# Attention and GEGLU on one core: 88 warm-up products of 32 columns, a block-diagonal v for batch 0, and clears moved between weight loads

## The chip, the core and the metric

The kernel runs on one core of a Trainium2 chip. A core has TensorE (PE, matrix products; its weight loads are listed as PEld), VectorE (DVE), ScalarE (ACT), GpSimd (POOL) and SyncE (SP), and 16 DMA engines that serve the queues of SP, ACT and POOL. The metric is the device time of one execution in microseconds (us), lower is better; the median over several executions is compared.

## What is computed

Dilated or plain sliding-window attention over 8 batches, 8 heads, 576 positions and head size 64, and then a feed-forward block with GELU gating. The second part takes the attention's output as 4608 tokens of 512.

```python
scores = scale * np.matmul(q, k.transpose(0, 1, 3, 2))
mask_plain = (rel >= 0) & (rel < 32)
mask_dil = (rel >= 0) & (rel < 32 * 4) & (rel % 4 == 0)
masks = np.stack([mask_plain if h < H // 2 else mask_dil for h in range(H)], axis=0)
attn = softmax(np.where(masks, scores, -1e9))
x = np.matmul(attn, v)            # as (4608, 512)
g = x @ w_gate                    # 512 -> 1536
val = x @ w_val
out = gelu(g) * val @ w_out       # 1536 -> 512
```

The first four heads have the plain window, the last four the dilated one. Inputs and output are float32; the kernel computes in float16 with float32 sums.

## The kernel before

**Pairs.** Two heads share the 128 partitions: 64 rows of keys of one head above 64 of the other. A batch has four pairs; pairs n = 0 and 1 of batch 0 are plain, 2 and 3 dilated. For each pair a fixed list of steps exists, named by one letter in the program strings: `S` scores on PE, `P` exp on ACT (line 466), `M` mask on DVE (471, not for batch 0, which has biases instead), `D` denominators on PE with a block-diagonal matrix of ones, `N` numerators on PE with v, `T` and `B` (reciprocal of the denominators by DVE transposes, 550 to 567) or `A` (the same on ACT as log and exp, 559 and 561), and `X`, the product of numerator and reciprocal on DVE (580), which writes the transposed tokens xT. `S1@6` is pair 1's scores in PSUM bank 6; the second number of `D` and `N` chooses one of two windows in PSUM.

**Block-diagonal or half.** For batches 1 to 7, k and v are spread into tiles whose 128x128 blocks are diagonal in the two heads, so that one full product serves both heads. Such a tile's other halves are cleared once (`zero`, line 194, two halves, each one memset of 64x576 float32) and stay clear; the casts (`cast_v`, line 249) write only the diagonal halves. There are three v tiles, `vraw[0..2]`, used by batch modulo 3, and two q/k tiles, by batch modulo 2. Batch 0 is short of time, so its pairs use plain, dense k and v, and each block takes two half products on 64 rows and 64 columns (L434 for S, L528 for N).

**The head.** Before the feed-forward's stream can begin, batch 0's attention runs alone. q and k of the plain heads are loaded (L654), cast (`c0` to `c3`, L351), turned on PE (`t0` to `t7`, L366 and L369) and copied back by DVE or ACT. Ahead of that PE runs `warm` (L637): 60 products of 64 columns on a tile of ones, and then six bias products (`bias_first`, L413) into banks 4 and 6. `b2` and `b3` are the bias products of pairs 2 and 3. `W` stands for filler products of 512 columns on ones (L643). The order of the steps on every engine is written by hand in `gates[0]`: each engine takes its share of it in that order. `G` loads ACT's GELU table; a number pops so many products of the feed-forward's list.

**The feed-forward.** 4608 tokens go in nine chunks of 512. Per chunk PE makes 12 blocks of gate and value (L589, 4 products each), ACT does the GELU (`g`, L743), DVE the product (`u`, L748), and then PE makes four output blocks (L596), stored by L607 or L609. Attention of later batches is woven into the output half of the chunks. Batch 1 is turned on PE (`t8` to `t15`) during chunk 0.

**POOL's queue.** POOL issues the loads of batch 0's dilated heads (L175) and v (`v_first`, L314 and L319), which come as float16 straight from a casting DMA; plain v of batch 0 comes as float32 through SP into `stage` (L237) and is cast by `cast_v_first`, one 128x576 copy for each of two groups g. Then POOL issues the weights: `load_w` (L152, two loads a part, six parts) and `load_wo` (L155). In `second()` (line 678) it goes on with part 4, batch 1's plain q and k (L682, "six"), part 5, its dilated q and k (L175, "eights"), the three output weights, then builds masks (L329 to L336, L132) and clears tiles of batch 1. Its further work for batch 1 (L266, spread of k) is queued behind that. `second_v()` clears the tiles of later batches.

Of the kernel before, what the change touches and what calls it, by code (L numbers as in the profile page):

```python
# [21 lines left out]
def kernel(  # L22
# [10 lines left out]
    nc = tc.nc  # L33
    B, H, S, D = q.shape
# [3 lines left out]
    NHP = H // 2  # L38
# [43 lines left out]
    vraw = [const.tile([P, 4 * NB2 * P], F16, tag=f"v{i}", name=f"v{i}") for i in range(3)]  # L82
# [64 lines left out]
    def load_w(*parts):  # L147

        for i in parts:
            for t, w in ((wg_t, moe_w_gate), (wv_t, moe_w_val)):  # L150
                src = w[:, WC[i][0] : WC[i][1]].rearrange("(kc p) n -> p kc n", p=P)
                nc.gpsimd.dma_start(out=t[i], in_=src)  # L152
# [24 lines left out]
    def blocks(t, plain):  # L177

        return t[:, (1 - plain) * 2 * NB2 * P : (2 - plain) * 2 * NB2 * P].rearrange("p (e c) -> p e c", c=P)

    def views(b):

        raw = qraw[b % 2]
        kt = raw[:, 1280 + 8 * NCL :]
        return (
            raw[:, 0:1280].rearrange("p (g c) -> p g c", g=2),
            raw[:, 1280 : 1280 + 8 * NCL].rearrange("p (g r i) -> p g r i", g=2, r=4),
            blocks(kt, 1),
            blocks(kt, 0),
            blocks(vraw[b % 3], 1),  # L190
            blocks(vraw[b % 3], 0),
        )

    def zero(t, eng=nc.gpsimd, half=(0, 1)):

        for x in half:
            part = t[64 * x : 64 * x + 64].bitcast(F32)
            eng.memset(part[:, :, 32 - 32 * x : 64 - 32 * x], 0.0)

    def st_of(i):  # L200
        return stage[:, 1280 * i : 1280 * i + 1280]
# [44 lines left out]
                in_=rows_[:, S - 64 : S].rearrange("g p d -> p g d"),  # L246
            )

    def cast_v(dst, i):
        st = st_of(i)[:, 0:1152].rearrange("p (e d) -> p e d", d=D)  # L250
        for g in range(2):
            at = slice(NB2 * g, NB2 * g + NB2)
            for x in range(2):
                half = slice(64 * x, 64 * x + 64)
                nc.gpsimd.tensor_copy(dst[half, at, half], st[half, at])  # L255
# [52 lines left out]

    def v_first(g):

        dst = vraw[0][:, 1152:2304].rearrange("p (e d) -> p e d", d=D)
        for x in range(2):
            half = slice(64 * x, 64 * x + 64)
            nc.gpsimd.dma_start(  # L314
                out=dst[half, 8 * g : 8 * g + 8].rearrange("p (i r) d -> p i (r d)", r=4),
                in_=v[0, HK + 2 * g + x, 0 : 4 * P].rearrange("(i p r) d -> p i (r d)", i=2, r=4),
            )
            if g == 0:
                nc.gpsimd.dma_start(out=dst[half, 16:18], in_=v[0, HK + x : H : 2, S - 64 : S].rearrange("g p d -> p g d"))  # L319

    def cast_v_first(eng, g):
        at = slice(576 * g, 576 * g + 576)
        copy(eng, vraw[0][:, at], st_of(0)[:, at])

    def two_masks():
        for x in range(2):
# [15 lines left out]
    def is_plain(n):  # L342
        return pair(n) < NHP // 2

    def copy(eng, dst, src):
        if eng == "act":
            nc.scalar.copy(dst, src)
        elif eng == "pool":
            nc.gpsimd.tensor_copy(dst, src)
        else:  # L350
            nc.vector.tensor_copy(dst, src)  # L351
# [130 lines left out]
    def two_mms(n, w0, lhs_of):  # L482

        mms = []
        pt = tiles["P", n]
        if lhs_of is None:
            groups = []
            for par in range(2):
                bl = two_blocks(n)
                bl = bl[par::2] if is_plain(n) else bl[4 * par : 4 * par + 4]  # L490
                for _, c0, t0, w in bl:
                    for o, l in cuts(w0 + t0, w):
                        p0, q0 = c0 + o, w0 + t0 + o
                        g = groups[-1] if groups else None
                        if g and g[2] == l and g[1] // 512 == q0 // 512 and g[4] == par:
                            last = g[3][-1]
                            if len(g[3]) == 1 or (
                                p0 - last[0] == last[0] - g[3][-2][0] and q0 - last[1] == last[1] - g[3][-2][1]
                            ):
                                g[3].append((p0, q0))  # L500
                                continue
                        groups.append((p0, q0, l, [(p0, q0)], par))
            for p0, q0, l, at, _ in groups:
                k = len(at)
                dp, dq = (at[1][0] - p0, at[1][1] - q0) if k > 1 else (l, l)
                mms.append((q0, at2(psf, q0, [[dq, k], [1, l]]), two_ones, at2(pt, p0, [[dp, k], [1, l]])))
        else:
            for e, c0, t0, w in two_blocks(n):
                for o, l in cuts(w0 + t0, w):
                    q0 = w0 + t0 + o  # L510
                    mms.append((q0, psf[:, q0 : q0 + l], lhs_of(e), pt[:, c0 + o : c0 + o + l]))
        if not is_plain(n):
            r = 0
            while r < 4:
                q0 = w0 + NCL * r + P
                k = sum((w0 + NCL * s + P) // 512 == q0 // 512 for s in range(r, 4))
                rest = two_ones if lhs_of is None else lhs_of(None)
                rhs = pt[:, LD - BK + 16 * r : LD - BK + 16 * (r + k)].rearrange("p (r i) -> p r i", i=16)
                mms.append((q0, at2(psf, q0, [[NCL, k], [1, 16]]), rest, rhs))
                r += k  # L520
        seen = set()
        for q0, o, lhs, rhs in mms:
            st = q0 // 512 not in seen
            seen.add(q0 // 512)
            if n < NHP and lhs_of is not None:
                for x in range(2):
                    half = slice(64 * x, 64 * x + 64)
                    nc.tensor.matmul(o[half], lhs[half], rhs[half], start=st, stop=True, skip_group_check=True)  # L528
            else:
                nc.tensor.matmul(o, lhs, rhs, start=st, stop=True, skip_group_check=True)  # L530
# [5 lines left out]
    def two_num(n, i):  # L536
        b, hp = n // NHP, n % 2
        _, _, _, _, vp, vd = tiles["two", b]
        if b == 0:
            vp, vd = (vraw[0][:, 1152 * i : 1152 * i + 1152].rearrange("p (e d) -> p e d", d=D) for i in range(2))  # L540
        if is_plain(n):
            two_mms(n, win(n, i), lambda e: vp[:, NB2 * hp + e, :])
        else:
            two_mms(n, win(n, i), lambda e: vd[:, 16 + hp if e is None else 8 * hp + e % 2 * 4 + e % 8 // 2, :])
        tiles["num", n] = win(n, i)
# [88 lines left out]
    def warm(n, bank, rows=P, cols=CH):  # L634

        for _ in range(n):
            nc.tensor.matmul(ps[0:rows, bank, 0:cols], ones[:, 0:rows], ones[:, 0:cols], start=True, stop=True)  # L637
# [26 lines left out]
    v_first(1)  # L664
    tiles["two", 0] = views(0)

    warm(60, 7, 32, 64)
    nc.vector.tensor_reduce(class_of, ident.rearrange("p (i r) -> p r i", r=4), axis=mybir.AxisListType.X, op=ALU.max)
    biases()
    zero(views(1)[2], nc.vector)  # L670
    bias_first(0, 4)
    bias_first(1, 6)
    load_w(0, 1)
    for g in range(2):
        cast_v_first("pool", g)
    load_w(2, 3)

    def second():

        load_w(4)  # L680
        for t, src in ((0, q), (1, k)):
            nc.gpsimd.dma_start(out=six[:, t].rearrange("p h r d -> p h (r d)"), in_=sixes(src, 1))  # L682
        load_w(5)
        load_eights(1)
        wo1 = [load_wo(i) for i in range(3)][1]
        two_masks()
        for t in views(1)[3:]:
            zero(t)
        tiles["two", 1] = views(1)
        gate["dma"] = wo1  # L690
        load_v(1, 1, True)
        load_v(1, 2, False)

    def second_v():
        for t in views(2)[2:4]:
            zero(t)
        cast_v(views(1)[4], 1)
        cast_v(views(1)[5], 2)
        for t in views(2)[4:] + views(3)[4:]:
            zero(t)  # L700

    def gate_banks(c, nb):
# [28 lines left out]
    def run_program(c, words, mms, banks):  # L731

        units = {"S": two_s, "M": two_m, "D": two_den, "N": two_num, "T": two_t, "B": two_b, "X": two_x, "A": two_a, "P": two_p_of, "t": turn_first, "c": cast_six, "W": idle, "b": bias_first}
        for word in words.split():
# [35 lines left out]

    gates = {
        0: (
            "c0@0 c1@0 t0@0@1 t1@1@0 W2@3@0 S0@4 P0 t4@0@1 c2@0 c3@0 W1@3@0 t5@1@0 t2@2@1 t3@3@0 D0@0 T0 B0 "
            "t6@1@1 t7@0@0 S1@6 P1 b2@2 S2@2 P2 D1@1 T1 B1 b3@0 S3@0 P3 N0@0 X0 D2@3 A2 D3@2 N2@1 X2 A3 N3@3 1 "
            "N1@2 X1 X3 G V 15 g0 u0 g1 u1 8 g2 u2 8 g3 u3 8 g4 u4 8 g5 u5 8 g6 u6 8 g7 u7 2 t8@4@1 t10@6@1 6 g8 "
            "u8 2 t9@5@0 t11@7@0 6 g9 u9 2 t12@4@1 t14@6@1 6 g10 u10 2 t13@5@1 t15@7@0 6 g11 u11"
        ),
        1: (
            "3 N7@0 e3@0 1 X7 1 G 8 g0 3 g1 u0 3 u1 2 g2 4 u2 4 g3 4 u3 4 g4 4 u4 4 g5 4 u5 4 g6 4 u6 4 g7 4 u7 4 "
# [111 lines left out]
```

## Time and profile before

| | |
|---|---|
| median of 8 runs | 337.83 us (337.36 to 338.57) |
| the profiled execution | 337.78 us |
| its span, first to last instruction | 336.1 us |
| PE busy | 329.0 us, 98% of the span |
| DVE, ACT, POOL busy | 164.3, 151.9, 148.4 us |
| DMA queues 0 and 1 | 6.79 MB and 39.99 MB |

PE is at work nearly all the time, and from about 20 us on without a break. A row of the chain of waits gives a start, a length and the work (or "issue", which is time in which the engine waited for nothing that the profile shows). A row of a timeline gives start, length, engine, line, operation, what it writes and reads, and in brackets the idle time before it and what ended that. Landing means the completion of a DMA. The head, up to 20.34 us, holds these other times that are used below:

| what | us |
|---|---|
| warm-up products, start to start | 0.053 |
| first copy of plain v landed, second, third, fourth | 12.09, 13.36, 15.59, 16.49 |
| v of the dilated pair 3 landed | 16.76 |
| first gate weights landed | 17.52 |
| output weights landed (three) | 40.56, 43.61, 46.69 |
| first product on the third output weights | 48.22 |
| batch 1's loads: plain q, k, dilated q, k | 30.96, 32.43, 36.64, 38.01 |
| PE turns them at | 33.81, 36.27, 38.73, 41.21 |

### The profile page before, as it was taken

The numbers are of one execution on the slowest core, as the hardware profiler recorded it, in microseconds if no ns is written. First come the engines' busy times: TensorE is split into PE (matmuls) and PEld (weight loads), VectorE is DVE, ScalarE is ACT, GpSimd is POOL, SyncE is SP. The second block draws the span as 40 slices with busy tenths as digits, with TensorE's granted clock in tenths as the row PEclk, the third lists the DMA queues.
The fourth block names the chain that finished last, engine by engine and source line by source line (L and its number), as shares of the span: only waits on it lengthen the run. The fifth ranks groups of instructions, "written<-read, shape, count | busy, mean of one in ns | idle before, by whom it ended". The sixth has DMA issues, their size and how long they took to land.

```text
span 336.1 us, 6358 instructions
## 1 busy us (share of the span) xinstructions
PE 329.0 (98%) x2447; PEld 171.3 (51%) x2447; DVE 164.3 (49%) x255; ACT 151.9 (45%) x226; POOL 148.4 (44%) x253
## 2 busy tenths in 40 slices
PE   7899999999999999999999999999999999999996
PEld 6654556444644465445654565445554444444443
DVE  6763454433833363345884297636695024303320
ACT  2663576535753566346633563346423243223321
POOL 8696998657518648549647701592000000000000
PEclk9999999999999999999999999999999999999999
DMA  8999997897979798899899327981100110020002
GB/s 191 183 194 197 205 178 165 231 183 189 247 196 171 176 247 175 220 227 182 238 204 215 112 90 191 184 196 64 62 3 0 64 63 0 2 94 31 0 33 94
DMA packets 109022, 47.90 MB, mean 143 GB/s; under 512 B 83648, under 2 KB 104512, under 8 KB 108992
## 3 DMA queue, kind: packets, MB, share of 16 engines
q1 hardware_dynamic: 97216, 39.99, 51.5%
q0 software_dynamic: 11216, 6.79, 14.1%
q10 hardware_dynamic: 560, 0.72, 0.8%
q8 instruction: 19, 0.31, 0.4%
q14 instruction: 11, 0.09, 0.1%
HBM read 37.75 MB, written 9.44 MB: 140 GB/s over the span
## 4 chain that ended last, share of the span: by engine, by line
PE 96%; ACT 1%; DVE 1%; issue 1%
PE ps L589 55%; PE ps L596 27%; PE ps L530 6%; PE ps L434 3%; PE ps L369 1%; PE ps L637 1%; PE ps L620 1%; PE ps L413 1%; ACT P L466 1%; PE ps L366 0%; ACT rb L561 0%; ACT lg L559 0%; DVE dense L351 0%; DVE xT L580 0%; DVE ones L66 0%
## 5 line engine op out<-in xcount | busy, mean ns | idle before, releaser
L748 DVE SCALAR_TENSOR_TENSOR u_all<-g,ps 128x512 f16<-128x512 f16 x108 | 73.9, 686 | 105.4 <-PE ps L589 96.5
L743 ACT ACTIVATE g<-ps 128x512 f16<-128x512 f32 x108 | 64.3, 597 | 115.6 <-PE ps L589 115.5
L589 PE MATMUL ps<-xT,wg 128*128 128x512 f16 x432 | 114.0, 379 | 0.2 <-DVE xT L580 0.2
L589 PE MATMUL ps<-xT,wv 128*128 128x512 f16 x432 | 113.3, 379 | 0.0
L596 PE MATMUL ps<-wo,u_all 128*128 128x512 f16 x420 | 100.9, 379 | 0.0
L589 PEld LDWEIGHTS <-wv 128*128 128x128 f16 x432 | 41.8, 98 | 48.6
L589 PEld LDWEIGHTS <-wg 128*128 128x128 f16 x432 | 41.5, 98 | 48.3 <-issue 0.4
L596 PEld LDWEIGHTS <-u_all 128*128 128x128 f16 x420 | 37.9, 97 | 38.0
L266 POOL COPY q<-dense 64x576 f16<-64x576 f16 (+2 forms) x70 | 38.4, 581 | 20.4 <-DMA dense<-s 16.4
L255 POOL CAST v<-stage 64x576 f16<-64x576 f32 x56 | 38.8, 693 | 3.6 <-DMA stage<-in_v_dram 0.8
L466 ACT ACTIVATE P<-ps 128x832 f16<-128x832 f32 (+1 forms) x32 | 26.8, 836 | 23.1 <-PE ps L434 22.9
L580 DVE TENSOR_TENSOR xT<-ps,rb 128x576 f16<-128x576 f32 x32 | 29.6, 932 | 11.3 <-ACT rb L561 7.0
L213 POOL CAST s<-stage 128x640 f16<-128x640 f32 x24 | 16.9, 732 | 37.1 <-DMA stage<-in_q_dram 21.6
L607 ACT ACTIVATE osb<-ps 128x512 f32<-128x512 f32 x34 | 20.2, 595 | 26.3 <-PE ps L596 26.2
L225 POOL CAST s<-stage 128x512 f16<-128x512 f32 x24 | 14.4, 627 | 10.2 <-DMA stage<-in_q_dram 5.4
L530 PEld LDWEIGHTS <-two_ones 128*128 128x128 f16 x176 | 13.8, 98 | 9.2 <-issue 1.5
L530 PE MATMUL ps<-P,two_ones 128*128 128x64 f16 (+8 forms) x176 | 16.5, 226 | 1.5 <-issue 1.4
L530 PEld LDWEIGHTS <-v 128*128 128x128 f16 x280 | 14.2, 98 | 5.4
L550 DVE STREAM_TRANSPOSE dt<-ps 128x576 f32<-128x576 f32 x19 | 14.7, 776 | 4.4 <-PE ps L530 4.2
L471 DVE TENSOR_TENSOR P<-P,two_d 128x768 f16<-128x768 f16 x14 | 9.3, 664 | 14.3 <-ACT P L466 14.2
L434 PEld LDWEIGHTS <-q 128*128 128x128 f16 x252 | 13.2, 98 | 5.1
L567 DVE STREAM_TRANSPOSE rb<-rc 128x576 f32<-128x576 f32 x19 | 14.7, 774 | 0.3
(70 smaller groups left out, 176.7 us busy)
## 6 DMA issues: line engine op xcount, KB each, us to landing
out_dram<-osb SPq DMA_DIRECT2D x35, 256.0 KB, 2.3
stage<-in_v_dram SPq DMA_DIRECT2D x32, 144.0 KB, 3.8
stage<-in_v_dram SPq DMA_DIRECT2D x28, 128.0 KB, 2.9
stage<-in_q_dram SPq DMA_DIRECT2D x24, 128.0 KB, 3.0
stage<-in_k_dram SPq DMA_DIRECT2D x24, 128.0 KB, 2.9
stage<-in_q_dram SPq DMA_DIRECT2D x6, 512.0 KB, 4.4
stage<-in_k_dram SPq DMA_DIRECT2D x6, 512.0 KB, 5.6
wg<-in_moe_w_gate_dram POOLq DMA_DIRECT2D x6, 256.0 KB, 7.7
```

What stands on the lines that cost most here:

```text
L213: nc.gpsimd.tensor_copy(s16[:, 1280 * t + 640 * g : 1280 * t + 640 * g + 640].rearrange("p (k c) -> p k c", k=5), st_of(i).rearrange("p (k ...
L255: nc.gpsimd.tensor_copy(dst[half, at, half], st[half, at])
L266: eng.tensor_copy(dst[half, :, :, half], src[half])
L434: nc.tensor.matmul(o, lhs, rhs, start=st, stop=True, skip_group_check=True)
L466: nc.scalar.activation(pt[:, 0 : src.shape[1]], src, AF.Exp, bias=0.0, scale=scale)
L530: nc.tensor.matmul(o, lhs, rhs, start=st, stop=True, skip_group_check=True)
L580: nc.vector.tensor_tensor(dst, num, rb, ALU.mult)
L589: nc.tensor.matmul(ps[:, bank, :], w[:, kc, ns], xT[kc][:, tok], start=first, stop=end)
L596: nc.tensor.matmul(ps[:, bank, :], u_all[:, fc, tb * P : (tb + 1) * P], wo_t[fc // 4][:, fc % 4, :], start=(fc == 0), stop=(fc == NNB - 1),)
L607: nc.scalar.activation(osb, ps[:, bank, :], AF.Copy, bias=0.0, scale=1.0 / USCALE)
L743: nc.scalar.activation(g, ps[:, gate_banks(c, args[0])[0], :], AF.Gelu)
L748: nc.vector.scalar_tensor_tensor(u_all[:, nb, :], tiles.pop(("g", nb)), USCALE, val, ALU.mult, ALU.mult)
```

## The change

There are five edits. The warm-up has 88 products of 32 columns in place of 60 of 64. Plain v of batch 0 goes into the block-diagonal tile `views(0)[4]`: its clear stands on DVE where a clear of batch 1's k stood, `cast_v` does it group by group (two 64x576 casts a group), and pairs 0 and 1 take full products for N. Dilated v of batch 0 moves to another part of `vraw[0]`, which is free of the plain block. All four clears of batch 1's tiles (eight memsets) stand right after `load_w(4)`, ahead of the "six" loads; before, three of them (six memsets) stood after the masks. `second_v` no longer clears the tile that DVE cleared. In the order of steps, both fillers `W` go, and D2 and A2 move ahead of N0 and X0.

```diff
-    def cast_v(dst, i):
+    def cast_v(dst, i, gs=(0, 1)):
         st = st_of(i)[:, 0:1152].rearrange("p (e d) -> p e d", d=D)
-        for g in range(2):
+        for g in gs:
...
-        dst = vraw[0][:, 1152:2304].rearrange("p (e d) -> p e d", d=D)
+        dst = vraw[0][:, 2304:3456].rearrange("p (e d) -> p e d", d=D)
...
-    def cast_v_first(eng, g):
-        at = slice(576 * g, 576 * g + 576)
-        copy(eng, vraw[0][:, at], st_of(0)[:, at])
...
-            if n < NHP and lhs_of is not None:
+            if n < NHP and lhs_of is not None and not is_plain(n):
...
-            vp, vd = (vraw[0][:, 1152 * i : 1152 * i + 1152].rearrange("p (e d) -> p e d", d=D) for i in range(2))
+            vd = vraw[0][:, 2304:3456].rearrange("p (e d) -> p e d", d=D)
...
-    warm(60, 7, 32, 64)
+    warm(88, 7, 32, 32)
...
-    zero(views(1)[2], nc.vector)
+    zero(views(0)[4], nc.vector)
...
-        cast_v_first("pool", g)
+        cast_v(views(0)[4], 0, (g,))
...
         load_w(4)
+        for t in views(1)[2:]:
+            zero(t)
...
         two_masks()
-        for t in views(1)[3:]:
-            zero(t)
...
-        for t in views(2)[4:] + views(3)[4:]:
+        for t in views(2)[4:] + views(3)[5:]:
             zero(t)
...
-            "c0@0 c1@0 t0@0@1 t1@1@0 W2@3@0 S0@4 P0 t4@0@1 c2@0 c3@0 W1@3@0 t5@1@0 t2@2@1 t3@3@0 D0@0 T0 B0 "
-            "t6@1@1 t7@0@0 S1@6 P1 b2@2 S2@2 P2 D1@1 T1 B1 b3@0 S3@0 P3 N0@0 X0 D2@3 A2 D3@2 N2@1 X2 A3 N3@3 1 "
+            "c0@0 c1@0 t0@0@1 t1@1@0 S0@4 P0 t4@0@1 c2@0 c3@0 t5@1@0 t2@2@1 t3@3@0 D0@0 T0 B0 t6@1@1 t7@0@0 S1@6 "
+            "P1 b2@2 S2@2 P2 D1@1 T1 B1 b3@0 S3@0 P3 D2@3 A2 N0@0 X0 D3@2 N2@1 X2 A3 N3@3 1 N1@2 X1 X3 G V 15 g0 "
```

## The prediction

> **What bounds the kernel now.** I read the page first: TensorE (PE) is busy 98% of the span and the chain that ended last is PE for 96%. So only what PE loses counts, and the next view is the chain of waits in order of time, cut to 0 to 60 us, for where it leaves PE.
>
> ```profile
> 4.92 1.50 PE ps L413 x6
> 6.42 0.97 PE ps L366 x12
> ...
> 12.12 0.87 ACT P L466
> 13.00 0.04 issue
> 13.04 0.35 PE ps L530 x2
> 13.39 1.36 issue
> 14.75 0.33 PE ps L530 x3
> 15.08 0.34 PE ps L413 x5
> 15.42 0.48 PE ps L434 x18
> 15.90 0.02 issue
> 15.92 0.81 ACT P L466
> ...
> 18.83 0.69 ACT rb L561
> 19.53 0.77 DVE xT L580
> 20.30 0.04 issue
> 20.34 13.54 PE ps L589 x62
> ```
>
> Columns: start, length, what. From 20.34 us on it is PE without a break. Before that runs the head, batch 0's attention, and what the head ends earlier the kernel ends earlier, if the later inputs keep up. At 13.39 the chain stands still for 1.36 us in the middle of D1, the five denominator products of pair 1: two run, three come at 14.75. Its input P1 was ready at 12.99. The waits of PE and the DMA queues (the second line cut to 11.5 to 13.6 us) say what it may be:
>
> ```profile
> PE ps L530 <- issue: 1.4, 1, 1.4
> ```
> ```profile
> q8 instruction: 19, 0.31, 0.4%
> ```
> ```profile
> q8 instruction: 1, 0.02, 4.4%
> ```
>
> No semaphore ended the wait, and an instruction packet travels just then (11.80 to 13.27 in the packet records). 19 packets are 16 KB each, and 2447 products and as many weight loads are 19.1 times 256: this queue feeds PE. I count PE's recorded instructions up to the gap, two per product: warm-up 120, biases 12, t0 and t1 24, W2 4, S0 36, t4 32, W1 2, t5 32, t2 and t3 24, D0 10, t6 and t7 64, S1 36, b2 10, S2 36, three loads and two products of D1: 447. So PE ran dry after number 447; the block before it ended at 447 - 256 = 191, inside S0, at 8.6 us. Fetch: passed at 8.6, packet at 11.80, first use at 14.75: 6.2 us.
>
> GpSimd (POOL) feeds PE's later inputs; its timeline:
>
> ```profile
> 13.50 0.66 POOL L349 CAST v<-stage 128x576 f16<-128x576 f32 x1
> 16.61 0.67 POOL L349 CAST v<-stage 128x576 f16<-128x576 f32 x1 [2.45 <-DMA stage<-in_v_dram]
> ...
> 31.24 0.74 POOL L155 DMA_DIRECT2D wo<-in_moe_w_out_dram  x1 [0.68 <-DMA s<-in_q_dram]
> ...
> 36.45 1.18 POOL L198 MEMSET q<- 64x576 f32 x2
> 37.66 2.40 POOL L198 MEMSET v<- 64x576 f32 x4
> 40.11 5.49 POOL L266 COPY q<-dense 64x576 f16<-64x576 f16 x10
> ```
>
> The clears at 36.45 hold up the copies into block-diagonal k, whose first four end at 42.69, 0.47 us before S4 on PE (43.16).
>
> [...] 96-column products stand 80 ns apart at 6.3 us and 42 ns at 9.8. [...] 16-column products here stand 25 ns apart, 32-column ones 29.
>
> **The change part by part.**
> *Warm-up.* 60 products of 64 columns stood 53.3 ns apart (1.54 to 4.73). 88 of 32 columns are not in the trace: 26.7 ns (32/64 of 53.3) at best, 53.3 at worst; I take 29, the warm 32-column spacing. End: 1.54 + 88 x 0.029 = 4.1 (3.9 to 6.2). Then the six bias products (1.38 us) need DVE's bias (4.16) and t0 needs DVE's cast (6.03), so t0 starts at 6.2 as now as long as the spacing is under about 36 ns. At 53.3 it starts 1.3 us later at half clock; as the clock would be released during it, I put that at 0.6 us of chain.
> *Block ends.* +28 products and -3 (W2, W1) are +50 instructions ahead of D1. Number 191 is now 176 + 12 + 3, in t0, at 6.2 us, 2.4 us earlier. Number 447 lies 50 earlier in the program, after the first load of b2, reached at 12.0. With the same 6.2 us the block is there at 12.4: a stall of 0.4 at b2, which feeds S2 and P2; ACT is busy with P1 to 12.99 anyway, so P2 moves from 13.02 to about 13.4 at most, and P3 does not depend on that. The latency is the unknown: the v loads, issued at 6.87 on another queue, show first packets 2.4 us later, so 5.4 to 6.2 is likely and 8.5 (the old arrival, 14.75) the far end.
> *Without the gap.* D1 runs at about 13.1. b3 needs bank 0 free from DVE's copy of t7, which ends at 14.05; DVE runs unbroken from 9.92 to there, so this is late next. b3 to P3 took 14.93 to 15.92 = 0.99; now 14.12 + 0.99 = 15.11 instead of 15.92: -0.81. W1 (0.32 on the chain at 9.17) held t5 0.15 us past its DMA (9.25); that copy starts DVE's unbroken run, so another -0.15 at most, and I count 0.1.
> *Order.* P3, lg, rb, lg, rb run back to back on ACT (15.92 to 19.53 = 3.6 us) and still do, from 15.0. D2 now stands before N0, so N0's wait for the v cast no longer stands ahead of what feeds A2; D2 ended with P3 before, so this alone is worth 0. N0 and N1 are 10 full products instead of 20 half ones that ran in pairs 42 ns apart: same time, 0. N1 after the second lg: 18.80 - 0.91 = 17.9. X1 follows X2 and ends at 19.3 to 19.4, and PE's stream begins there, not at 20.34: about -1.0.
> *What else must be there by then.* v halves: two casts of 0.69 in place of one of 0.66, twice. The first pair ends at 14.9, before N0 (15.4). For the second the half of x=0 lands at 15.59 and that of x=1 at 16.49, so it ends at 17.3 (18.0 if both are awaited), before N1. Weight issue then starts at 17.3 to 18.0, not 17.2. N3's v lands at 16.76, wg0 at 17.52: both before their use. Second fetch: block end 703 falls just after N1, reached at 18.3, fetched by 12.4 + 6.2 = 18.6; X2 ends at 18.3 and three products follow before X1 is through, so 0 to 0.2 is lost.
> *Clears.* DVE's two are equal (538 ns, other tile). POOL clears eight halves, 8 x 0.61 = 4.9 us, after load_w(4), from about 21.7 to 26.6; six of those were at 36.45, two are new, two go in second_v. Queued behind: both six loads, w5, both eights, three wo. Cover: the weights queued by then keep the DMA engines going until w4 lands at 29.5; the six loads issued at 26.6 need about 2.6 us (3.17 to 5.80, the first POOL load's first packet), so 29.2: no gap, 0.3 to spare; a starved queue would delay wo, of which the tightest (wo2, landing 46.69, used 48.2) has 1.5 us, 0.5 after a gain of 1.0. Cost 0. In exchange the k copies start when t11 is through (37.2 then) and the masks end (37.7), and end by 40.3, before S4 at 42.1. Without this move they would give back about 0.6 us.
>
> Sum: -0.8 - 0.1 - 0.1 (X1 right behind X2) = -1.0. The profiled execution took 337.78, 1.7 over its span of 336.1, and the median is 337.83, so the forecast is 336.8 for either.
>
> **The rivals.** Differences under 0.2% (0.7 us) can't be told from none.
> *A, forecast, 0.56:* 336.8, own range 336.4 to 337.1. For: a gap that no engine's work explains, and a fetch that is asked for 2.4 us earlier.
> *B, part of it, 0.12:* 32-column products stand near 53 ns: head +0.6, gain about 0.5: 337.3. Against: 29 ns when warm.
> *C, hidden, 0.09:* N1, wg0, the v casts and the second fetch all meet at about 18, or the wo loads come late; the gain goes there: 337.7.
> *D, slower, 0.15:* the block's arrival is set by the loaded DMA engines and not by when it is asked for, so it comes at 14.75 again. PE now stands at b2 and S2 instead of D1; S2, D1, b3 and S3 all follow: P3 starts at 14.75 + 2.1 = 16.85, +0.9: 338.7. It turns slower than before from an arrival of 13.8 on (13.8 + 2.1 = 15.9). For: the packet waited 3.2 us; DMA is above 90% busy from 2 us on. Against: 2.4 us of notice.
> *E, slower, 0.08:* the warm-up ends at 4.1, PE idles 0.5 us before t0 and W2 is gone, so [...] half clock lasts 3.4 us more: PE's 2.9 us of work from 7.4 becomes some 5, of which about 1 reaches P3: 338.8.
>
> **How the numbers follow.** A is faster by over 0.2% nine times in ten, B one time in three, C never; D and E are slower. Faster 0.50 + 0.04 = 0.54, same 0.06 + 0.08 + 0.09 = 0.23, slower 0.15 + 0.08 = 0.23. The range runs from A's best (all 0.15 of t5, no second fetch, the spacing at its least: 336.3) into D (arrival at 14.2: 15.92 becomes 16.3, 338.2).
>
> **What would show it.** Right: no gap at D1; PE's first unbroken weight product near 19.3; the first fetch packet at about 9; P3 near 15.0. Warm-up products 27 to 36 ns apart. Wrong: a gap at b2 or S2 that ends near 14.75 (D); 96-column products still 80 ns apart after 8 us (E); t0 past 7 us (B); PE waiting for DMA at t8, t12 or wo (C).

## The result and the profile after

| | median us | lowest to highest | runs |
|---|---|---|---|
| before | 337.80 | 337.20 to 338.94 | 32 |
| after | 340.03 | 339.33 to 340.93 | 11 |

The ratio is 1.0066 [1.0055, 1.0076]: 2.2 us slower, where 1.0 us faster was forecast. The profiled execution of after took 340.31 us over a span of 338.6. The lines of before that the views name stand 4 higher in after: L434 is L430, L369 is L365, L366 is L362, L530 is L526, L589 is L585. Four executions among all those used below (385, 700, 1940 and 1963 us) lie far from the rest and are left out of the ratios.

The chain of waits of after, cut to the first 60 us (columns: start, length, what):

```profile
3.17 6.99 DMA xT<-in_q_dram
10.15 0.04 issue
10.19 1.17 PE ps L365 x32
...
15.06 0.76 PE ps L409 x5
15.82 0.78 PE ps L430 x18
16.60 0.82 PE ps L526 x5
...
18.61 0.81 ACT P L462
...
22.04 0.77 DVE xT L576
22.81 0.04 issue
22.86 13.54 PE ps L585 x62
```

Two things stand here side by side. The denominator products (L526) run as five in 0.82 us without a break: the stall of 1.36 us that the forecast wanted gone is gone. But the unbroken stream begins at 22.86 us, not at 20.34: 2.52 later. From its start to the end of the program it is 317.45 us, before 317.44 (each profiled execution's time less the stream's start), so in these two executions the whole loss lies in the head, batch 0's attention, and none behind it.

Inside the head the new order of events shows twice. The chain now begins with a load: PE's t4 (L365, 32 transposes) waits for the q load of the dilated heads until 10.19; before it started at 8.72. And PE's work up to there is slow: 18 score products (L430) in 0.78 us where the same row before had 0.48. PE's timeline and its list of waits say how it came to t4:

```profile
1.54 2.53 PE L633 MATMUL ps<-ones 128*32 128x32 f16 x88 [1.54 <-DVE ones L66]
...
6.09 0.92 PE L362 MATMUL ps<-ident,s 96*128 96x96 f16 x12 [0.98 <-DVE s L347]
...
7.86 0.89 PE L430 MATMUL ps<-q,dense 64*64 64x96 f16 x18 [0.85 <-DVE dense L347]
10.19 1.17 PE L365 MATMUL ps<-ident,xT 72*64 72x72 f16 x32 [1.45 <-DMA xT<-in_q_dram]
```
```profile
PE ps L365 <- DMA xT<-in_q_dram: 1.5, 1, 1.5
PE ps L362 <- DVE s L347: 1.0, 1, 1.0
PE ps L430 <- DVE dense L347: 0.8, 1, 0.8
```

The warm-up is over after 2.53 us (before, the same row is 3.38 long), and then PE stands still 0.98, 0.85 and 1.45 us before t4. Of these three pauses before's list has only the one for the dense tile, of 0.3. What the clock did meanwhile is in the windows of 3.5 us (columns: length, busy us and count of PE, weight load, DVE, ACT, POOL, then granted clock, DMA share, GB/s). First before, two windows:

```profile
5.00:8.50 3.50, 3.21 (x32) 1.94 (x32) 2.57 (x5) 0.64 (x1) 3.50 (x6) 1.00 1.20 223
8.50:12.00 3.50, 3.49 (x116) 2.89 (x108) 2.70 (x6) 2.67 (x4) 2.95 (x6) 1.00 1.46 184
```

and after:

```profile
5.00:8.50 3.50, 1.61 (x32) 1.21 (x30) 2.94 (x6) 0.64 (x1) 3.50 (x6) 0.92 1.18 221
8.50:12.00 3.50, 2.05 (x50) 1.81 (x44) 1.05 (x2) 1.51 (x3) 1.64 (x4) 0.50 1.38 192
12.00:15.50 3.50, 3.50 (x65) 2.92 (x63) 3.24 (x7) 1.67 (x3) 3.44 (x6) 0.50 1.39 185
15.50:19.00 3.50, 3.50 (x60) 2.77 (x58) 1.83 (x5) 1.67 (x3) 3.38 (x6) 0.62 1.44 194
```

Between 5.0 and 8.5 PE was busy 1.61 us, before 3.21. Then the clock falls to half: the clock records give full clock for 4.49 to 7.90, half for 7.90 to 18.14 (three periods of 3.41 us), then full. Before it was full from 7.52 on without a break. From 12.0 to 19.0 PE is busy 7.00 of 7.00 us and gets 125 products through; before, from 8.5, it got 116 through in half of that time. The clock column must be read with care: ahead of the first record it prints 1.00 where the array is slow too. In before, whose first record stands at 7.52, the 96-column products of L366 stand 80 ns apart at 6.3 us and 42 to 43 at 9.9: the array ran at half its later pace while the column printed 1.00. That state is called cold below.

The third thing is the load. The instruction packet that travels 11.80 to 13.27 in before, during PE's stall, travels 6.65 to 7.89 here by the packet records. The DMA queues of 6.5 to 8.2 us have it as one packet (columns: packets, MB, share of 16 engines):

```profile
q8 instruction: 1, 0.02, 4.6%
```

Its 1.24 us are 4.6% of 16 engines over 1.7 us, so it kept one engine busy. The q load that t4 waits for lands in 16 parts: 15 of them by 8.31 (before all by 8.63), the last at 10.15. One part is 1.84 us behind the rest.

POOL's timeline shows the clears and what stands behind them:

```profile
21.90 2.40 POOL L198 MEMSET q<- 64x576 f32 x4
24.34 2.40 POOL L198 MEMSET v<- 64x576 f32 x4
26.69 0.69 POOL L680 DMA_DIRECT2D s<-in_q_dram  x1
...
30.99 2.29 POOL L155 DMA_DIRECT2D wo<-in_moe_w_out_dram  x3
```

Eight memsets end at 26.7 and the "six" loads are issued then, as the forecast had it; they land at 31.06 and 32.49, before 30.96 and 32.43. The three wo loads land at 42.21, 44.76 and 48.14: 1.2 to 1.7 us later than before.

So there were three candidates: the clock, the late q load, and the order and clears, which the forecast had set at nothing.

### The profile page after: what moved, and what is told of

It is laid out like the page before. It is cut to its first block, busy times and chain, and to the rows that moved or that the text cites. A ratio compares the mean times of both kernels' runs of the same rounds, so it can differ in the third digit from the quotient of the medians.

```text
span 338.6 us, 6369 instructions
## 1 busy us (share of the span) xinstructions
PE 330.0 (97%) x2452; PEld 172.1 (51%) x2452; DVE 163.9 (48%) x255; ACT 151.9 (45%) x226; POOL 149.9 (44%) x255
## 4 chain that ended last, share of the span: by engine, by line
PE 95%; DMA 2%; DVE 1%; ACT 1%; POOL 0%; issue 0%; DVEq 0%
PE ps L585 55%; PE ps L592 27%; PE ps L526 7%; PE ps L430 3%; DMA xT<-in_q_dram 2%; PE ps L365 1%; PE ps L616 1%; ACT lg L555 0%; PE ps L362 0%; ACT P L462 0%; DVE dt L546 0%; DVE xT L576 0%; PE ps L409 0%; ACT rb L557 0%; POOL band L116 0%
## 5 line engine op out<-in xcount | busy, mean ns | idle before, releaser
L585 PE MATMUL ps<-xT,wg 128*128 128x512 f16 x432 | 114.0, 379 | 0.2 <-DVE xT L576 0.2
L585 PE MATMUL ps<-xT,wv 128*128 128x512 f16 x432 | 113.3, 379 | 0.0
L585 PEld LDWEIGHTS <-wv 128*128 128x128 f16 x432 | 41.7, 98 | 48.7
L585 PEld LDWEIGHTS <-wg 128*128 128x128 f16 x432 | 41.5, 98 | 48.3 <-issue 0.4
L266 POOL COPY q<-dense 64x576 f16<-64x576 f16 (+2 forms) x70 | 38.5, 581 | 25.5 <-DMA dense<-s 16.6
L255 POOL CAST v<-stage 64x576 f16<-64x576 f32 x60 | 41.3, 688 | 3.1
L576 DVE TENSOR_TENSOR xT<-ps,rb 128x576 f16<-128x576 f32 x32 | 29.7, 933 | 11.9 <-ACT rb L557 7.0
L526 PEld LDWEIGHTS <-v 128*128 128x128 f16 x300 | 15.2, 98 | 6.0 <-issue 0.6
L526 PEld LDWEIGHTS <-two_ones 128*128 128x128 f16 x176 | 14.1, 100 | 8.1 <-issue 0.5
L526 PE MATMUL ps<-P,two_ones 128*128 128x64 f16 (+8 forms) x176 | 17.1, 232 | 0.1
L526 PE MATMUL ps<-P,v 128*128 128x96 f16 (+1 forms) x300 | 15.8, 199 | 0.3 <-ACT lg L555 0.3
L430 PEld LDWEIGHTS <-q 128*128 128x128 f16 x252 | 13.2, 98 | 5.1
```

The costliest lines, as they stand in the source:

```text
L266: eng.tensor_copy(dst[half, :, :, half], src[half])
L576: nc.vector.tensor_tensor(dst, num, rb, ALU.mult)
L585: nc.tensor.matmul(ps[:, bank, :], w[:, kc, ns], xT[kc][:, tok], start=first, stop=end)
```

## The experiments

All kernels below compute the whole result; the edits change warm-up, order or gate only. Each was timed in five rounds beside the kernel before, so the ratios are to before on the same chip. "Clock" is the mean granted clock of an execution. Where two experiments are compared I take the difference of their ratios times 337.8 us, with an interval from the two intervals (root of the summed squares).

### First four: warm-up alone, fillers alone

a_warm60 is after with the old warm-up:

```diff
-    warm(88, 7, 32, 32)
+    warm(60, 7, 32, 64)
```

> The changed kernel with the old warm-up: 60 products of 64 columns; everything else of the change stays. Theory 1 (the earlier instruction block sits on one DMA engine amid the q and k loads of the dilated heads): the block is asked for late again, t4 starts at about 8.7 us instead of 10.19, the gap at D1 is back, time 337.3 to 338.2 us. Theory 2 (PE at half clock from 7.9 to 18.1 us is the whole loss[...]): PE is busy until 4.9 again, so partly mended, 338 to 339 us. Theory 3 (v's casts, the order of D2 or the clears cost it): stays at 340 us.

338.94 us (337.26 to 340.84, 22 runs), ratio 1.003 [1.0015, 1.0044]. Half of the loss goes with the old warm-up, half stays. In the profile (338.62) the q load lands at 8.51 at the latest and the packet travels at 11.21, so the load is on time again, and PE's list of waits has no row of "issue" either. But this kernel has no fillers: 14 of 22 executions have a mean clock of 0.990 or less, and the profiled one is at half from 9.32 to 16.15. b_nofill below has the same trouble.

b_warm88 is before with the new warm-up alone:

```diff
-    warm(60, 7, 32, 64)
+    warm(88, 7, 32, 32)
```

> The kernel before with only the new warm-up, 88 products of 32 columns; fillers stay. Theory 1: the block's packet travels at 6.5 to 8 us, one engine's share of the first q load lands 1.2 to 1.8 us after the others, t4 starts past 10 us, time 339.2 to 340.3 us. Theory 2: the fillers keep the clock up, at most 338.3 us. Theory 3: 337.8 us, as before.

340.45 us (337.28 to 341.80, 15 runs), ratio 1.0072 [1.0055, 1.0089]. This one line is enough to make the whole loss. PE's timeline:

```profile
1.54 2.53 PE L637 MATMUL ps<-ones 128*32 128x32 f16 x88 [1.54 <-DVE ones L66]
...
7.86 0.56 PE L434 MATMUL ps<-q,dense 64*64 64x96 f16 x18 [0.42 <-DVE dense L351]
10.35 0.45 PE L369 MATMUL ps<-ident,xT 72*64 72x72 f16 x16 [1.93 <-DMA xT<-in_q_dram]
```

The packet travels 6.78 to 7.99, 15 parts of the q load land by 8.38 and the last at 10.31, and t4 waits 1.93 us: as in after, without any of its other edits. The clock falls to half for 11.86 to 15.27. The window of 3.5 us ahead of that, with most of the wait in it:

```profile
8.50:12.00 3.50, 1.65 (x45) 1.33 (x46) 0.91 (x2) 1.56 (x3) 1.37 (x4) 0.98 1.44 175
```

PE is busy for 1.65 us of it, so here the pause for the late load stands right ahead of the fall. In after the clock had fallen at 7.90, before PE began to wait for the load at 8.74.

a_fill is after with the two fillers back in the order:

```diff
-... t1@1@0 S0@4 P0 t4@0@1 c2@0 c3@0 t5@1@0 ...
+... t1@1@0 W2@3@0 S0@4 P0 t4@0@1 c2@0 c3@0 W1@3@0 t5@1@0 ...
```

> The changed kernel with both fillers W (two and one products of 512 columns) put back at their old places. Theory 1: t4 still waits past 10 us, 339.2 to 340 us, at most the half-clock share of 0.5 us comes back. Theory 2: the clock holds, 337.0 to 338.0 us. Theory 3: 340 us.

340.32 us (337.54 to 341.51, 22 runs), ratio 1.0066 [1.0048, 1.0083]. The fillers do not heal it. Its executions fall in two groups, three of 22 between 337.5 and 337.8, most between 339 and 341.5, and the profiled one (337.65) is of the good group: full clock, q load in by 8.71, stream at 19.83. So one program differs by 3 us from one execution to another; only a good one was traced, so where the others lose is not shown.

b_nofill is before without the fillers:

```diff
-... t1@1@0 W2@3@0 S0@4 P0 t4@0@1 c2@0 c3@0 W1@3@0 t5@1@0 ...
+... t1@1@0 S0@4 P0 t4@0@1 c2@0 c3@0 t5@1@0 ...
```

> The kernel before without the fillers W. Theory 1: the block comes when it came, 337.5 to 338.1 us. Theory 2: the clock falls after 7.9 us, above 338.3 us, with a mean clock of about 0.985. Theory 3: 337.8 us.

338.75 us (337.26 to 339.46, 14 runs), ratio 1.0013 [0.9999, 1.0028]. Two groups again: five executions at a clock of 0.995 or more take 337.3 to 337.6, eight at 0.990 or less take 338.7 to 339.5 (one, of 338.61, reads 1.0). So without the fillers the old warm-up fails to keep the clock up in about half the executions, and that costs some 1.4 us (medians of the two groups, 338.90 and 337.52).

### Second four: how long, how many, which order

b_w60c32 shortens the warm-up of before without adding products, so that the packet stays where it was:

```diff
-    warm(60, 7, 32, 64)
+    warm(60, 7, 32, 32)
```

> The kernel before with 60 products of 32 columns: as many instructions as before, half the columns, so the warm-up ends near 3.3 us. Theory 1 (it is the number of PE instructions ahead of the first block end that moves the block's packet into the q and k loads): the packet stays at 10.5 to 12 us and executions at full clock take 337.2 to 338.2 us. Theory 2 (it is PE's shorter busy time): as slow as with 88 products of 32 columns, 340 us, also at full clock.

340.07 us (339.25 to 340.40, 5 runs), ratio 1.0063 [1.0051, 1.0075]. The packet travels at 11.77 and the q load is in by 8.40, on time. The loss is as large as after's all the same: too short a warm-up is enough, with the load on time and the fillers in place. PE's timeline of the profiled execution (339.37):

```profile
13.58 0.90 PE L434 MATMUL ps<-q,dense 64*64 64x96 f16 x18
...
15.16 0.85 PE L434 MATMUL ps<-q,dense 64*64 64x96 f16 x18
...
16.95 0.53 PE L434 MATMUL ps<-q,dense 64*64 64x96 f16 x18
```

The same 18 products take 0.90 and 0.85 us, then 0.53: the first record of full clock is at 16.4. Yet this execution's mean clock reads 0.999: the time before the first release (the first full clock) is not in that figure. A mean clock near 1 therefore does not say that the clock came early; only the clock records of a traced execution do.

b_w88c64 has the new count and the old width, on the kernel before:

```diff
-    warm(60, 7, 32, 64)
+    warm(88, 7, 32, 64)
```

> The kernel before with 88 products of 64 columns: as many instructions as in the change, but PE is busy without a break until about 6.2 us. Theory 1: the packet travels at about 7 to 8.5 us, the q and k loads' last shares land late, 339.5 us or more, about 0.5 of it from t0 starting later. Theory 2: the clock holds in every execution, at most 338.6 us.

337.42 us (336.82 to 337.74, 13 runs), ratio 0.9988 [0.998, 0.9996], and every execution at a clock of 0.998 or more. Against b_warm88, the same number of instructions with products of half the length, that is -0.0084: -2.8 us (2.2 to 3.5). PE's timeline:

```profile
8.22 0.56 PE L434 MATMUL ps<-q,dense 64*64 64x96 f16 x18 [0.42 <-DVE dense L351]
8.70 0.45 PE L369 MATMUL ps<-ident,xT 72*64 72x72 f16 x16
...
13.96 0.52 PE L530 MATMUL ps<-P,two_ones 128*128 128x384 f16 x5
...
19.89 0.59 PE L589 MATMUL ps<-xT,wg 128*128 128x512 f16 x2 [0.16 <-DVE xT L580]
```

t4 starts at 8.70 without a wait (q load in by 8.55, packet 7.96 to 9.24), the five denominator products run unbroken at 13.96, and the stream begins 0.45 earlier than before.

a_w60_fill is a_fill with `warm(60, 7, 32, 64)`: what is left of the change without its warm-up and without the filler removal.

> The changed kernel with the old warm-up and both fillers: what stays of the change is v block-diagonal, the clears, and D2 and A2 ahead of N0. Theory 1 and 2 alike: 337.3 to 338.1 us, no difference from before, since the two causes are gone. Theory 3 (one of these three parts costs time of its own): above 338.5 us.

338.45 us median of 13 (lowest 336.98; 338.22 without the one of 1963 us), ratio 1.0008 [0.9996, 1.0019]. v, clears and order bring nothing measurable. The profiled execution (337.18) is one of the fastest: its stream begins at 19.29, 1.05 us earlier than before, and 0.6 of that reaches the end. Most of the 1.05 is the stall at D1, which is short here:

```profile
13.69 0.33 PE L526 MATMUL ps<-P,two_ones 128*128 128x288 f16 x3 [0.35 <-issue]
```

The packet travels at 10.41 to 11.92, 1.4 us earlier than in before (11.80), though as many products stand ahead of it. So the packet's time also differs between programs with the same count of products ahead of D1; why is not shown.

a_fill_order is a_fill with the late load given more time: t2, t3 and S1 stand ahead of what needs it.

```diff
-S0@4 P0 t4@0@1 c2@0 c3@0 W1@3@0 t5@1@0 t2@2@1 t3@3@0 D0@0 T0 B0 t6@1@1 t7@0@0 S1@6 P1 ...
+S0@4 P0 c2@0 c3@0 W1@3@0 t2@2@1 t3@3@0 t4@0@1 t5@1@0 D0@0 S1@6 T0 B0 t6@1@1 t7@0@0 P1 ...
```

> The changed kernel with the fillers, and t2, t3 ahead of t4, t5, and S1 ahead of t6, t7: PE has pair 1's plain work to do while the dilated heads' q is on its way. Theory 1: the late share is covered in part, 1 to 2 us under the changed kernel with fillers alone (340.3): 338 to 339.3 us. If the late load is not what PE loses, 340.3 us or more.

337.90 us (337.07 to 339.79, 22 runs), ratio 1.0018 [1.0005, 1.003]; against a_fill -0.0048, -1.6 us (0.9 to 2.3). With the short warm-up kept, other work over the wait for the load brings most of it back. This order changes the load's cover and PE's idle time together, so it doesn't part the two.

### Third four: parting clock, packet and instruction block

a_w166c32_fill keeps the 32-column products and the fillers, and makes the warm-up as long in time as that of b_w88c64, by more products:

```diff
-    warm(88, 7, 32, 32)
+    warm(166, 7, 32, 32)
```

> The changed kernel with both fillers and 166 products of 32 columns, at 28 ns each 4.6 us of PE. Clock theory: length and not width counts, so the clock is up by 8 us, 336.9 to 338.0 us. If products of 32 columns do not count as work for the clock: 340 us or more, as with 88 of them.

338.68 us (338.31 to 340.61, 14 runs), ratio 1.0039 [1.0024, 1.0054]. Against a_fill -0.0027, -0.9 us (0.1 to 1.7); by the medians -1.6. The warm-up keeps PE busy 4.61 us and the clock holds in the profile, but number 191 of the forecast's count now lies inside the warm-up, near 4.1 us (an estimate from 4.61 us for 166 products), and the packet travels at 6.08 to 7.27, amid the loads:

```profile
8.33 0.56 PE L430 MATMUL ps<-q,dense 64*64 64x96 f16 x18 [0.42 <-DVE dense L347]
9.78 0.45 PE L365 MATMUL ps<-ident,xT 72*64 72x72 f16 x16 [0.90 <-DMA xT<-in_q_dram]
```

Fifteen parts of the q load land by 8.30 and the last at 9.74, and t4 waits 0.90 us; the k load beside it lands by 8.93 and at 10.92. Four of the 14 executions read a mean clock of 0.990, at 339.6 to 340.6 us: with the load late, even 4.6 us of warm-up did not always keep the clock. The result lies between the two expectations.

a_w88c64_fill is the same kernel with `warm(88, 7, 32, 64)`: as long a warm-up, with 78 products fewer.

> The changed kernel with both fillers and 88 products of 64 columns, so PE is busy to 6.2 us and the block is still asked for early. Clock theory (the loss is the time for which PE runs at half clock, set by how long the warm-up keeps PE busy): every execution reaches full clock by 8 us, 336.9 to 337.5 us, and what the head gains beyond that is lost at pair 8's scores near 80 us, which wait for POOL's copy of line 306. Theory 1 (the block's packet amid the loads is the main loss): 339 us or more.

337.72 us (337.20 to 338.87, 14 runs), ratio 1.0001 [0.9988, 1.0013]; against a_w166c32_fill -0.0038, -1.3 us (0.6 to 1.9). Its packet travels 7.70 to 8.80, its q load is in by 8.58, and t4 waits 0.20:

```profile
8.62 0.45 PE L365 MATMUL ps<-ident,xT 72*64 72x72 f16 x16 [0.20 <-DMA xT<-in_q_dram]
```

Both have a full clock in the profile, where they differ by 1.0 us (338.33 and 337.33). The 1.3 holds some loss of clock too, in a_w166c32_fill's four executions; over those with a mean clock of 0.998 or more the means are 338.62 and 337.81, 0.8 apart. I put the packet's place at 0.8 to 1.0 us by these figures, an estimate, since 78 products more also move every later block.

b_w60c96 lengthens the warm-up of before by width alone, so that the packet stays late:

```diff
-    warm(60, 7, 32, 64)
+    warm(60, 7, 32, 96)
```

> The kernel before with 60 products of 96 columns: the instruction count of before, PE busy to about 6.3 us. Both theories: full clock early in every execution, the gap at D1 still there: 337.4 to 337.9 us; against 88 products of 64 columns (337.42) the difference is what the earlier block is worth, 0 to 0.4 us.

338.12 us (337.60 to 338.90, 13 runs), ratio 1.0007 [0.9995, 1.0018]. Packet at 11.88, the stall at D1 there as before, stream at 20.35. b_w88c64 against it has a clock that came as early (5.46 and 5.33 in the profiles) and an earlier packet: -0.0019, -0.6 us (0.2 to 1.1). That is what the forecast's own step, D1 without its stall, is worth here. It is net of a loss: in b_w88c64 the third and fourth loads of the dilated heads land their last part at 10.98 and 12.02, 1.0 and 1.1 us after the other 15, and PE waits 0.58 us for the fourth.

a_best_gate0 is a_w88c64_fill with SP's later loads released by the first output weight instead of the second:

```diff
-        wo1 = [load_wo(i) for i in range(3)][1]
+        wo0 = [load_wo(i) for i in range(3)][0]
...
-        gate["dma"] = wo1
+        gate["dma"] = wo0
```

> The changed kernel with both fillers, 88 products of 64 columns, and SP's loads of batch 1's v let go when the first output weight has landed, not the second, so that SP and POOL are earlier for batch 2. If the wait at pair 8's scores caps the gain: 336.3 to 336.9 us. If the output weights, now in competition with v, bind first: 337.2 us or more.

337.55 us (336.83 to 338.30, 13 runs), ratio 0.999 [0.998, 1.0]: not told apart from a_w88c64_fill.

### Last two: where the head's gain goes

a_w88c64 is after with `warm(88, 7, 32, 64)` and no fillers: the whole change with a long warm-up.

> The changed kernel with 88 products of 64 columns and without fillers: one edit away from the change. If the length of the warm-up alone decides the clock: 337.4 to 338.0 us, as with the fillers. If the fillers keep the clock up after it: a share of the executions shows a mean clock of 0.985 to 0.99 and 338.5 us or more.

338.41 us (337.04 to 339.32, 14 runs), ratio 1.0013 [1.0001, 1.0025]. That is above the range expected for a clock that holds, although 13 of 14 executions have a mean clock of 0.998 or more. The profiled one (338.69), at full clock from 6.12, loses elsewhere. It starts its stream at 19.61, 0.73 earlier than before, and yet ends 0.91 later than before. Its PE timeline near 80 us, where pair 8, the first of batch 2, takes its scores:

```profile
79.83 0.34 PE L430 MATMUL ps<-q 128*128 128x96 f16 x4 [0.38 <-POOL q L266]
80.97 0.33 PE L430 MATMUL ps<-q 128*128 128x80 f16 x5 [0.80 <-POOL q L306]
```

and POOL's timeline there:

```profile
80.63 0.29 POOL L306 COPY q<-q 128x128 f16<-128x128 f16 x1
```

In before, POOL's timeline and PE's are:

```profile
79.39 0.29 POOL L306 COPY q<-q 128x128 f16<-128x128 f16 x1
```
```profile
79.89 0.51 PE L434 MATMUL ps<-q 128*128 128x96 f16 x9
```

The copy was ready at 79.68. The first four of the nine products do not need it (they run ahead of it in a_w88c64); the fifth starts at 80.06 in before's trace. That is 0.4 us of slack, which no wait in the profile of before shows. A stream 0.7 us early runs into it even if the copy stays where it was, and here the copy is 1.24 later.

b_w88c64_gate0 is b_w88c64 with the gate's edit of a_best_gate0, to release that copy's loads earlier.

> The kernel before with 88 products of 64 columns and SP's loads of batch 1's v let go at the first output weight. If the scores of pair 8 near 80 us, which wait for POOL's copy of line 306, cap what the head gains, POOL is there 1 us or more earlier and the 0.3 us lost since the head come back: 336.9 to 337.2 us. If not: 337.4 us, as without it.

337.51 us median (lowest 336.71), ratio 0.9986 [0.998, 0.9993]. In its profile, of the lowest execution, the copy starts at 77.48, no wait is left behind 20 us, and a stream from 19.26 ends the program at 336.71, 1.07 earlier than before. The gate removed the wait; the earlier stream (19.26 against 19.89 in b_w88c64) is not its doing, since the head is the same program: full clock came at 4.48 in this execution and at 5.46 in that one. On the median it is not told apart from b_w88c64. These two have the lowest ratios found; they beat before by 0.1%, less than the 0.2% I call measurable for one comparison, though both intervals exclude 1.

What the profiled executions say together (us; "tail" is the time less the stream's start):

| kernel | stream starts | time | tail | later wait of PE |
|---|---|---|---|---|
| before | 20.34 | 337.78 | 317.44 | none new |
| after | 22.86 | 340.31 | 317.45 | none new |
| b_w60c96 | 20.35 | 337.79 | 317.44 | none new |
| b_w88c64 | 19.89 | 337.65 | 317.76 | 0.2 for L306 |
| a_fill_order | 19.70 | 338.05 | 318.35 | 0.8 for L306 |
| a_w88c64 | 19.61 | 338.69 | 319.08 | 0.4 and 0.8 for L266, L306 |
| a_w60_fill | 19.29 | 337.18 | 317.89 | for the second output weights, to 44.42 |
| b_w88c64_gate0 | 19.26 | 336.71 | 317.45 | none new |

## Why the prediction was wrong

**The step that failed: "Warm-up".** The forecast asked of it only when it ends and whether t0 is held up, found that t0 starts at 6.2 "as now as long as the spacing is under about 36 ns", and so put nothing. The spacing was near enough: taken at 29 ns, it was 26.9 (88 starts from 1.54 to 3.88), and t0 started at 6.09. But it took the clock as given, and the length of the warm-up is part of what holds the clock. Busy for 1.8 us (b_w60c32) the array came to full clock only at 16.4; for 2.5 us (after, b_warm88, a_fill) it fell back, or stayed cold, in most executions, going by their clocks and times (half of after's executions read a mean clock of 1.0 at 339.3 to 340.0 us; a late first release as in b_w60c32 would give that, but none of these was traced); for 3.4 us (before) it held with the fillers and failed in about half the executions without (b_nofill); for 4.5 us (b_w88c64, a_w88c64) it held in 26 of 27, going by a mean clock of 0.998 or more. The warm-up is not alone in it, since 4.6 us in a_w166c32_fill, with the load late, failed in four of 14.

What the traces have in common is PE's idle time: in the three in which the clock fell, PE was busy for 1.5 us (after, 4.49 to 7.90), 2.2 (a_warm60, 5.91 to 9.32) and 1.5 (b_warm88, 8.45 to 11.86) of the 3.41 us ahead of the fall. A short warm-up, missing fillers and a late load all add such idle time (waits of 0.98, 0.85 and 1.45 us in after, 0.85 in a_warm60, 1.93 in b_warm88). The products of 32 columns were chosen as if a warm-up were a number of instructions, and are shorter by just what mattered.

The clock records show changes at 4.49, 7.90 and 18.14 us in after: once 3.41 apart and once three times that. When full clock first comes differs between executions of one and the same head: 5.46 us in b_w88c64, 4.48 in b_w88c64_gate0. One and the same program makes two groups of times (b_nofill, medians 337.52 and 338.90 us; a_fill); that the moment of the clock's changes sorts them is not shown, as each program has one traced execution.

**Rival E named it and sized it too small.** It had the pause before t0, the missing W2 and half clock for 3.4 us, at 338.8 and with a chance of 0.08. Measured was half clock for 10.2 us, three times 3.41, at 340.0; the 3.4 us came in b_warm88 (11.86 to 15.27). E's own sign came too: at 11.3 us the 96-column products of t2 and t3 stood 80 ns apart. In the second of these three stretches PE had no pause (columns: length, busy us and count, granted clock, DMA share, GB/s):

```profile
11.30:14.70 3.40, 3.40 (x66) 0.50 1.40 193
```

Why full clock did not come after that is not shown by a run. 47 of the 66 products in that stretch are transposes (L365 x35, L362 x12), for 2.0 us of it. Their time sorts the traces so far: take the stretches of 3.41 us at half clock in which PE had no pause (ahead of a first record, counted back from it in steps of 3.41, an estimate from the records' spacing). Where transposes took 1.5 us or more, half clock went on: after from 11.3, a_warm60 from 9.3, b_w60c32 from 6.2 and from 9.6. Where they took 1.3 or less, full clock followed: b_warm88 from 11.9 with 1.27 us, before from 4.1 with 0.94, after from 14.7 with none. That the transposes are the cause is not shown: no kernel here varies that share alone.

**"Block ends" was right in direction, and its delay and one term were wrong.** The packet came earlier (6.65 against 11.80 us) with 50 instructions more ahead of D1, and the stall at D1 went; rival D, in which the block comes at 14.75 again, is refuted. That a packet is asked for when PE passes the end of the block before was the author's estimate, from 19 packets for 4894 instructions, and is not shown. The forecast took the delay from the block's end to the packet as fixed, 3.2 us as in before (8.6 to 11.80), and so had the packet at "about 9". In after number 191 stands at 6.10 and the packet starts at 6.65, 0.55 us on; over the traces the delay runs from 0.2 (a_fill) to 3.4 us (b_w60c96), and what sets it is not shown. What the sum lacked is what comes with a packet among the loads of q and k (6.65 to 7.89 in after, 6.78 to 7.99 in b_warm88, 6.08 to 7.27 in a_w166c32_fill): it keeps one engine busy for 1.24 us in after, and t4 waits for the last of its load's 16 parts, which lands at 10.15, 1.84 behind the other 15. That was worth 0.8 to 1.0 us by the estimate from a_w166c32_fill and a_w88c64_fill. With the packet at 7.70 or later the first q load was in time (8.58 in a_w88c64_fill, 8.55 in b_w88c64), and later loads had the part that lags (by 1.0 and 1.1 us in b_w88c64). That the packet makes the one part late was not shown: which engine took the packet was not traced, and the lag varied from 0.5 us (a_fill's profiled execution) to 1.9 (b_warm88).

**The size of the gain.** "-0.8" for the gap was -0.6 (0.2 to 1.1) at the end of the program by b_w88c64 against b_w60c96; at the stream's start it was 0.46 (19.89 against 20.35).

**"What the head ends earlier the kernel ends earlier, if the later inputs keep up."** They do not all keep up. I checked k of batch 1 and the wo loads, and not batch 2: pair 8's copy L306 has 0.4 us of slack. In b_w88c64 the copy is also 0.2 us later, and of a head early by 0.45 there is 0.13 left at the end; in a_w88c64 it becomes a loss.

**Order, v block-diagonal, clears: "Cost 0".** For the "six" loads the figure held (0.06 to 0.10 us later). But the wo loads come 1.2 to 1.7 us later in after, and the late head does not account for it: in a_w60_fill, whose head is early, they come at 41.84, 44.38 and 47.18, 0.5 to 1.3 later than before, and PE waits for the second. Rival C, in which the wo loads come late, had this. Together with the order and v these edits brought nothing: a_w88c64_fill 1.0001 against 0.9988 for b_w88c64 without them, +0.0013, or 0.4 us (-0.1 to 0.9). Even with a longer warm-up the change was not faster than before.

**How the loss is made up.** t4 starts 1.47 late (10.19 against 8.72), and from t4 to the stream it is 12.67 instead of 11.62 us although a stall of 1.36 has gone: 1.47 + 1.05 = 2.52. The late load and the clock are not independent, as b_warm88 suggests, where the wait for the load stands right ahead of the clock's fall. So I don't divide the 2.2 us of the medians further than the figures above: 0.8 to 1.0 for the packet alone at full clock, and the whole loss for the short warm-up alone with the packet late (b_w60c32).

## What to carry to other kernels

Measure a warm-up in microseconds of busy array, not in products, give it margin (here 26 of 27 executions with 4.5 us read a mean clock of 0.998 or more; with 3.4 us and no fillers, about half read 0.995 or more), and look at PE's pauses behind it: one program, b_nofill, had two groups of times, 337.5 and 338.9 us. Before instructions are added ahead of a stall in which an instruction packet travels, look at which loads the packet may fall among: with 50 instructions more it travelled from 6.65 us instead of 11.80 here, among the loads of q and k. And before a gain at the start is booked at the end, look at the slack of every later input, also those that no wait shows because they now come just in time.

## What was not expected of the hardware

- In the traces in which the instruction packet of 16 KB travelled among the loads (6.1 to 8.0 us), one of the 16 parts of a load landed up to 1.9 us after the other 15: 8.38 and 10.31 in b_warm88, 8.31 and 10.15 in after, 8.30 and 9.74 in a_w166c32_fill.
- The mean granted clock leaves out the time before the first release: b_w60c32's profiled execution reads 0.999 and was cold until 16.4 us. Durations of equal products (0.90 against 0.53 us) tell what it hides.
- Half clock lasted through a stretch in which PE was busy from end to end (11.3 to 14.7 us in after), with transposes for 2.0 us of it.
- Warm-up products of 32 columns stood 27 ns apart ahead of the first clock record (after), those of 64 columns 53 (before): half the time each, and 60 of them kept PE busy for 1.8 us (b_w60c32) instead of 3.4 (before).
